# A new order of the steps in a one-core RWKV-7 and GELU kernel, all five engines scheduled by one list

## The chip, the cores and the metric

The kernel runs on one core of a Trainium2 chip. Its time is the device time of one execution in microseconds. Each kernel is run several times and the median counts.

## The reference

Two parts, one behind the other. First a recurrence over 768 time steps, for 4 batches of 8 heads with 40 channels; each head keeps a 40x40 state:

```
for t in range(S):
    y[:, :, t] = einsum('bhd,bhde->bhe', rt, state)
    Sa = einsum('bhde,bhe->bhd', state, at)
    state = state * wt - einsum('bhd,bhe->bhde', Sa, bt) + einsum('bhd,bhe->bhde', vt, kt)
```

Then y, as a matrix x of 3072 tokens by 320, goes through an MLP with 2048 hidden units: `gelu(x @ w_in) @ w_out`, with the exact GELU. Inputs of the recurrence are fp32; w_in and w_out come as 64-bit floats, which the kernel turns into fp32 on the chip.

## The kernel before, in words

The 768 time steps are cut into 12 chunks (c = 0 to 11) of 64. Within a chunk the recurrence is written as matrix products: products of the decayed a, b, k, r and v rows, the inverse of a triangular 64x64 matrix for each of 32 pairs of batch and head, and an update of the state. The MLP for a chunk's 256 tokens comes one chunk later.

Nothing schedules the work but one list. `order` (line 19) returns some 1,470 tokens; the loop at the end of the kernel performs them one by one through `perform` (line 114), and each engine runs its instructions in exactly that order. So a token is a step with its numbers: `sm.7` is step `sm` of chunk 7, `mh.7.2` the step `mh` of chunk 7, part 2. Engines meet through semaphores only. The steps that the text speaks of:

- **Loads, issued by SP**: `Lw La Lb Lk Lr LV Lv Lbt Lwt Lkt` (lines 447 to 486) bring rows of the inputs of a chunk, `Lf` and `Lf5` (537, 547) pieces of w_in, `Ls` (577) of w_out. `ox.c.x` (1241) moves parts of y between halves of the partitions, 5 or 6 DMAs a token, 11 a chunk. `so` and `sz` (1417, 1422) write the output; a last letter `a` or `s` names the queue (ACT or SP).
- **Conversion of the weights**, 18 units u (0 to 9 of w_in, 10 to 17 of w_out). `cp`, `cm`, `cs` on DVE and `ce` on ACT take a unit apart; then either `cv.u` puts it together on DVE (two instructions, lines 636 and 637), or `cl.u` and `cn.u` on ACT and `cg.u` on POOL do it (659, 660). Unit 1 goes over PE (`cx`, `cy`).
- **Decays and transposes**: `lg` `ec` `ew` `lt` `en` on ACT (logarithm and exponentials), `pw` on DVE (a scan), `ta tb tk tr tv tw` transposes (PE and a copy for the first chunks, DVE from chunk 3 on), `sa sb sn kc` on DVE and `sk` on POOL or DVE scale by the decays.
- **Small products on PE**, 32 matmuls each, which the trace counts as 64: `nm vm am` (64 columns), `av xm sm pk pb` (104 columns), `ym` (64), `jm km` (32x32 tiles), and `cu` (the sums of the logarithms).
- **Around them**: `nk vk ak` mask a product on DVE (line 865); `nd` (ACT) and `nx` (DVE) bring the triangular blocks to the tile Nb; `iz` and `ic.c.j0.j1` on POOL invert them in 31 steps of two instructions (962 and 964); `wx` and `tc_` on DVE turn the result, `wa`, `wb` and `jc` on ACT copy. `xc0` and `xc1` (ACT, DVE) copy out behind `xm`, `kt0` and `kt1` behind `km`, `sc.c.g` (DVE, 1176) masks behind `sm`, `yc` (ACT) copies behind `ym`; `oa`, `om`, `od` (DVE) update the state and write y into `xt`, `oc`, `ot` (ACT) and `tn` (DVE) turn the state for the next `ym`.
- **MLP**: `mh.c.p` (1303), 8 a chunk, 10 matmuls each (20 in the trace) of 64 rows with two in the array at once; `ge.c.q` (ACT, 1313) applies GELU to two of them. Then `x W_out` in seven products of half size, `m1` to `m7` (1344), 8 matmuls each (16 in the trace) of the full array, with sums and differences on DVE before (`s1` to `s4`) and behind (`e1` to `e6`, partly ACT). `ws.n` makes the sums of w_out once, on DVE. Chunk 0 uses four plain pieces, `pm.0.n` (1429), instead.
- **warm** tokens are matmuls on constants whose result nobody reads; there are 13 and a first one.

The recurrence goes from chunk to chunk by this path: `od` of the last chunk, `xm`, `xc0`/`xc1`, `sm`, `sc`, `pb`, `oa`, `od`. The inverse of a chunk, `nm` to `nk`, `nd`, `nx`, `ic`, `wx`, `tc_`, `jm`, `km`, `sm`, doesn't need the state and is begun a chunk ahead. PSUM is four tiles that `take` hands out in turn (line 177): a PE step that takes one waits until its last user's readers are done.

Of the kernel before, what the change touches and what calls it, by code (L numbers as in the profile page):

```python
# [18 lines left out]
def order(chunks, first_seven):  # L19
    return """  # L20
        Lw.0 of_half_set warm_set pads_a.1 warm_first pads_a.0 stripes_set Lw.1 bias_set pads_rows.1 pads_VR.1
        sums_mask pads_w.0 pads_extra.3 La.0 pads_VR.0 identity pads_extra.0 first_ones.0 Lf.0.0.0 pads_w.1
        Tt_zero warm.4.5 Lb.0 lg.0 onward_set pads_r.0 lg.1 wT.0 upper_mask Lf.1.1.0 first_ones.1 pads_extra.1
        cu.0 Lf.0.1.0 pads_rows.0 Lf.1.0.0 wT.1 ec.0 Lb.1 ew.0 ta.0 La.1 sb.0 sa.0 tb.0 Lf.3.0.0 Lf.3.1.0 cm.0
        sn.0 cp.0 nm.0 cl.1 Lk.0 warm.4.18 nk.0 Lr.0 cm.1 qi.0.p cu.1 cp.1 cn.1 qt cn.0 warm.4.10 ec.1 qm.0 ew.1
        sb.1 LV.0 parity_set ce.1 qi.1.v cl.0 tb.1 ce.0 cx.1 qz.0 sn.1 qb.0.0.v qc.0 cs.0 cg.0 Lf.2.0.0 qb.0.1.a
        ta.1 cm.3 Lf.0.0.1 cs.1 qm.1 Lf5.1.1 sa.1 pads_extra.2 cy.1 sk.0.p nm.1 qa.1 qz.1 iz.1 tk.0 nk.1 qb.1.1.a
        qc.1 tr.0 qb.1.0.v nd.1 cp.3 kc.0 nx.1 qm.2 Lf.0.1.1 ce.3 ic.1.0.4 rc.0 cs.3 Lw.2 tv.0 cv.3 qc.2 qz.2
        am.0 Lf5.1.0 vc.0 qa.2 ic.1.4.8 qb.2.0.v qb.2.1.a qm.3 Lf.2.0.1 cp.5 ak.0 ce.5 Lf.2.1.1 vm.0 cm.5
        Lf.2.1.0 ic.1.8.12 qz.3 warm.4.6 qa.3 Ls.1 qb.3.0.v warm.4.29 cs.5 vk.0 lg.2 Lk.1 qb.3.1.a cv.5 qc.3 qm.4  # L30
        Lf5.0.1 ic.1.12.16 cp.7 ce.7 av.0 qa.4 cm.2 qx Ls.0 cm.7 cp.2 ql warm.4.21 ic.1.16.20 xc1.0 LV.1
        warm.4.13 ce.2 cs.7 xc0.0 cu.2 cv.7 jm.0 Lf5.0.0 sk.1.v warm.4.8 jc.0 cm.9 warm.4.22 pads_r.1 La.2 km.0
        ic.1.20.24 ec.2 warm.4.24 kt1.0 Lr.1 cs.2 kt0.0 warm.4.3 cv.2 sm.0 Lf.1.1.1 Ls.5 cp.9 warm.4.25
        ic.1.24.28 ce.9 cp.4 sc.0.1 ce.4 pk.0 Lb.2 sc.0.0 cs.9 tr.1 Lf.1.0.1 cm.4 cv.9 Lf.3.1.1 pb.0 rc.1
        unused.v Lf.3.0.1 ic.1.28.31 wT.2 om.0.0 tk.1 om.0.1 od.0.0 ox.0.0 od.0.1 tv.1 cs.4 oc.0 cv.4 ew.2 ta.2
        vc.1 sb.2 cp.6 kc.1 tb.2 unused.a sa.2 ox.0.1 ce.6 am.1 sn.2 cs.6 vm.1 cm.6 ot.0.0 wx.1 nm.2 cv.6 iz.2
        mh.0.0 cm.8 cp.8 Ls.3 ak.1 ce.8 cn.8 cs.8 Ls.7 cl.8 mh.0.1 nk.2 ot.0.1 cg.8 Ls.2 vk.1 wa.1.1 nd.2 mh.0.2
        Lk.2 nx.2 cp.10 ge.0.0 ic.2.0.4 tn.0 av.1 Lr.2 ce.10 cm.10 wa.1.0 ym.1 Ls.4 sk.2.v mh.0.3 yc.1 ic.2.4.8
        cs.10 LV.2 cm.11 tc_.1 tk.2 cp.11 ge.0.1 Ls.11 cv.10 xm.1 ce.11 Ls.6 kc.2 ic.2.8.12 jm.1 cm.12 Ls.9 wb.1
        cp.12 cs.11 mh.0.4 xc1.1 Ls.8 cv.11 xc0.1 jc.1 Ls.10 ce.12 tr.2 cp.13 cs.12 km.1 La.3 rc.2 ic.2.12.16  # L40
        cm.13 tv.2 ce.13 cv.12 kt1.1 Lwt.3 mh.0.6 vc.2 cm.14 cp.14 cs.13 kt0.1 cl.14 cv.13 Lw.3 mh.0.7 ce.14
        cn.14 cs.14 cg.14 am.2 cp.15 cm.15 ce.15 vm.2 Ls.14 mh.0.5 vk.2 ak.2 Ls.15 ic.2.16.20 pm.0.0 cs.15 Ls.13
        cv.15 Ls.12 ge.0.3 ge.0.2 cm.17 Lk.4 ta.3 cn.17 sm.1 ic.2.20.24 tw.3 pm.0.1 lg.3 Lv.3 cp.16 cp.17 sc.1.1
        ce.17 cm.16 ce.16 cs.17 Lr.3 cl.17 sc.1.0 cs.16 pk.1 cv.16 cg.17 pb.1 Lb.3 cu.3 oa.1.1 pm.0.3 ec.3 Lbt.3
        ic.2.24.28 oa.1.0 od.1.1 od.1.0 om.1.1 oc.1 om.1.0 ot.1.1 warm.4.23 ox.1.1 ot.1.0 pc.0.1 ic.2.28.31 av.2
        tn.1 lt.3 ym.2 wx.2 tb.3 pm.0.2 wb.2 yc.2 tc_.2 so.0.1 pw.3 ox.1.0 ew.3 jm.2 pc.0.0 unused.r xm.2 sa.3
        jc.2 wa.2.0 tr.3 km.2 xc0.2 Lk.3 mh.1.0 en.3 wa.2.1 La.4 sn.3 kt1.2 kt0.2 tv.3 nm.3 xc1.2 sk.3.p sm.2
        Lkt.3 nk.3 iz.3 nd.3 mh.1.4 nx.3 sc.2.0 ic.3.0.4 mh.1.5 sc.2.1 ta.4 pk.2 ge.1.2 ic.3.4.8 tk.3 pb.2 Lr.4
        kc.3 mh.1.2 oa.2.1 ws.0 Lbt.4 mh.1.6 ic.3.8.12 ws.1 od.2.1 mh.1.1 Lwt.4 oa.2.0 ws.2 mh.1.3 LV.3 od.2.0
        oc.2 tr.4 ge.1.0 mh.1.7 ws.3 Lw.4 ic.3.12.16 ot.2.0 om.2.0 vm.3 ge.1.3 am.3 ge.1.1 vk.3 so.0.0 m1.1  # L50
        ot.2.1 s1.1 om.2.1 m2.1 ak.3 ox.2.1 ic.3.16.20 tn.2 av.3 s2.1 e1.1 sb.3 ym.3 tb.4 m5.1 yc.3 Lkt.4 tw.4
        ic.3.20.24 m6.1 s3.1 lg.4 e2.1 ox.2.0 s4.1 lt.4 xm.3 pw.4 m3.1 Lb.4 ew.4 ic.3.24.28 xc1.3 m7.1 e3.1 en.4
        e4.1 La.5 tk.4 m4.1 e5.1 ic.3.28.31 Lr.5 sn.4 mh.2.4 e6.1 sa.4 so.1.1 wx.3 mh.2.5 kc.4 wb.3 LV.4 xc0.3
        tc_.3 cu.4 nm.4 Lv.4 ec.4 jm.3 sk.4.p nk.4 mh.2.2 ge.2.2 Lw.5 iz.4 nd.4 wa.3.0 nx.4 mh.2.3 jc.3 wa.3.1
# [1413 lines left out]
```

## Time and profile before

| | us |
|---|---|
| median of the runs (3) | 644.49 |
| lowest, highest | 643.8, 646.84 |
| the profiled execution | 638.89 |
| its span, from first to last instruction | 637.2 |
| PE busy in the span | 621.2 |
| DVE, POOL, ACT busy | 463.5, 383.5, 311.6 |
| first mh step (mh.0.0) begins | 76.2 |
| nm.3 begins | 140.25 |
| last matmul ends | 632.65 |

The times of a profile are those of its one execution, counted from the first instruction. Busy time of PE is that of matmuls; PEld loads their weights and overlaps it. Matmuls are pipelined and their ends are modelled, so the distance from start to start says more than the length of one.

### The profile page before, as it was taken

How to read it: one execution, taken by the hardware profiler on the slowest of the kernel's cores; microseconds unless marked ns; L12 is line 12 of the kernel's file. 1: busy time of each engine (PE TensorE's matmuls, PEld its weight loads, DVE VectorE, ACT ScalarE, POOL GpSimd, SP SyncE). 2: the span in 40 equal slices, each digit the busy share in tenths (PEclk: the TensorE clock that was granted, in tenths of full speed). 3: DMA queues.
4: the chain of work that ended last, by engine and by line, in shares of the span. 5: the costliest groups of instructions: out<-in, count | busy, mean ns of one | idle time of the engine just before them, and what ended most of it. 6: DMA issues, size and time to landing. Idle time of an engine off the chain costs nothing.

```text
span 637.2 us, 27873 instructions
## 1 busy us (share of the span) xinstructions
PE 621.2 (97%) x12424; PEld 548.8 (86%) x12424; DVE 463.5 (73%) x555; ACT 311.6 (49%) x441; POOL 383.5 (60%) x783
## 2 busy tenths in 40 slices
PE   7989999999999999999999999999999999999997
PEld 4676887678998998998988998998998998989996
DVE  1889989989986996986867887984964784833212
ACT  3566684582645454735546536437563275241010
POOL 4568779728867848818958718958918808810000
PEclk9899999999999999999999999999999999999999
DMA  9998587947576458268366466368344440210100
GB/s 152 168 172 162 121 180 160 175 96 123 95 144 114 85 105 149 41 121 143 66 104 116 92 113 123 70 116 153 72 87 96 84 85 4 42 25 3 37 6 21
DMA packets 246898, 64.06 MB, mean 101 GB/s; under 512 B 228380, under 2 KB 243644, under 8 KB 246780
## 3 DMA queue, kind: packets, MB, share of 16 engines
q1 hardware_dynamic: 246340, 62.01, 52.8%
q8 instruction: 97, 1.59, 1.1%
q10 hardware_dynamic: 440, 0.29, 0.2%
q14 instruction: 21, 0.17, 0.1%
HBM read 54.39 MB, written 3.93 MB: 92 GB/s over the span
## 4 chain that ended last, share of the span: by engine, by line
PE 83%; DVE 5%; POOL 3%; ACT 3%; SPq 2%; issue 2%; DMA 1%; DVEq 0%; POOLq 0%; ACTq 0%
PE bank L1308 31%; PE bank L1347 27%; PE bank L194 24%; POOL W L964 2%; POOL tmp L962 2%; DVE conv L628 1%; SPq L447 1%; DMA bk_rows<-in_b_dram 1%; PE bank L1429 1%; SPq L577 1%; DVE SM L1176 1%; DVE conv L636 1%; DMA w_out_sb<-in_moe_w_out_dram 1%; ACT conv L1264 1%; ACT conv L614 0%
## 5 line engine op out<-in xcount | busy, mean ns | idle before, releaser
L1308 PE MATMUL bank<-xt,w_in_sb 64*128 64x256 f32 x1920 | 221.7, 382 | 0.0
L962 POOL TENSOR_TENSOR tmp<-W,Nb 128x126 f32<-128x126 f32 (+22 forms) x341 | 162.4, 476 | 74.4 <-DVE Nb L928 49.0
L1308 PEld LDWEIGHTS bank<-xt,w_in_sb 64*128 64x128 f32 x1920 | 182.0, 187 | 23.2 <-issue 0.8
L964 POOL TENSOR_TENSOR W<-W,tmp 128x126 f32<-128x126 f32 (+22 forms) x341 | 170.7, 501 | 26.7
L1347 PE MATMUL bank<-w_out_sb,gt 128*128 128x160 f32 x704 | 101.1, 301 | 0.0
L1347 PEld LDWEIGHTS bank<-w_out_sb,gt 128*128 128x128 f32 x704 | 96.6, 190 | 2.5 <-issue 1.2
L1313 ACT ACTIVATE gt<-bank 128x1024 f32<-128x1024 f32 x48 | 48.6, 1025 | 85.5 <-PE bank L1308 80.9
L1264 ACT COPY conv<-st 32x128 f32<-32x128 f32 (+2 forms) x55 | 28.0, 509 | 39.5 <-DVE st L1258 31.6
L1176 DVE TENSOR_TENSOR SM<-bank,upper 128x832 f32<-128x832 f32 (+1 forms) x24 | 23.0, 985 | 22.0 <-PE bank L194 21.9
L1300 DVE TENSOR_TENSOR os<-os,bank 128x160 f32<-128x160 f32 x44 | 13.9, 316 | 24.5 <-PE bank L1347 18.2
L1347 PE MATMUL bank<-extra,conv 128*128 128x160 f32 x208 | 30.3, 300 | 0.0
L1300 DVE TENSOR_TENSOR conv<-gt 128x1024 f32<-128x1024 f32 x11 | 14.1, 1286 | 21.6 <-ACT gt L1313 21.6
L1347 PEld LDWEIGHTS bank<-extra,conv 128*128 128x128 f32 x208 | 28.9, 190 | 0.1
L1228 DVE TENSOR_TENSOR st<-bank,st 128x832 f32<-128x832 f32 (+1 forms) x22 | 20.9, 986 | 8.0 <-PE bank L194 8.0
L790 POOL TENSOR_TENSOR bk_rows<-bk_rows,part 128x640 f32<-128x640 f32 x9 | 15.0, 1666 | 19.3 <-DMA bk_rows<-in_k_dram 15.6
L947 POOL MEMSET W<- 128x512 f32 x11 | 5.8, 526 | 34.6 <-DVE Tt L933 34.6
L722 DVE TENSOR_TENSOR_SCAN kT<-spare,kT 128x256 f32<-128x256 f32 x36 | 25.5, 768 | 1.4 <-ACT kT L715 1.4
L1347 PE MATMUL bank<-extra,gt 128*128 128x160 f32 x176 | 25.8, 300 | 0.0
L1347 PEld LDWEIGHTS bank<-extra,gt 128*128 128x128 f32 x176 | 24.5, 190 | 0.1
L1313 ACT ACT_TABLE_LOAD x18 | 23.1, 1283 | 0.3
L1347 PE MATMUL bank<-extra,SM 128*128 128x160 f32 x144 | 21.2, 300 | 0.0
L194 PEld LDWEIGHTS bank<-SM,Tt 64*64 64x64 f32 x768 | 17.2, 133 | 4.1 <-issue 2.3
(218 smaller groups left out, 1113.9 us busy)
## 6 DMA issues: line engine op xcount, KB each, us to landing
bk_rows<-in_b_dram SPq DMA_DIRECT2D x24, 160.0 KB
bk_rows<-in_k_dram SPq DMA_DIRECT2D x24, 160.0 KB
out_dram<-os SPq DMA_DIRECT2D x46, 80.0 KB
VR<-in_v_dram SPq DMA_DIRECT2D x22, 160.0 KB
w_tile<-in_w_dram SPq DMA_DIRECT2D x36, 80.0 KB
a_pairs<-in_a_dram SPq DMA_DIRECT2D x18, 144.0 KB
v_pairs<-in_w_dram SPq DMA_DIRECT2D x18, 144.0 KB
v_pairs<-in_v_dram SPq DMA_DIRECT2D x18, 144.0 KB
```

The costliest lines, as they stand in the source:

```text
L194: nc.tensor.matmul(o, lhsT, rhs, start=first, stop=True, skip_group_check=True)
L722: nc.vector.tensor_tensor_scan(logs[:, at:at + n], onward, logs[:, at:at + n], 0.0, ALU.mult, ALU.add)
L790: (nc.vector if q == "v" else nc.gpsimd).tensor_tensor(to, rows(k_of(c)), decays(c), ALU.mult)
L962: nc.gpsimd.tensor_tensor(t, W[:, BL // 2 - rows:, rest:rest + 1].to_broadcast([P, rows, rest]), Nb[:, rest:rest + 1, :rest].to_broadcast( ...
L964: nc.gpsimd.tensor_tensor(own, own, t, ALU.add)
L1176: nc.vector.tensor_tensor(SM[:, g, :, :, cols], pair_of(f"S{c}_", g).rearrange("p x i c -> p i x c")[:, :, :, cols], kept, ALU.mult)
L1228: nc.vector.tensor_tensor(to, pair_of(f"QY{c}_", g)[:, :, :, cols], to, ALU.add)
L1264: nc.scalar.copy(apart.rearrange("p e i g d -> p (e i g) d")[to_rows, :, to_col:to_col + n], st.rearrange("p e i g c -> p (e i g) c")[rows ...
L1300: nc.vector.tensor_tensor(to, one_, other, how)
L1308: nc.tensor.matmul(ph[:, x, s], w_in_sb[half(x), kt, p * P:(p + 1) * P], xt[half(x), kt], start=kt == 0, stop=kt == NK - 1)
L1313: nc.scalar.activation(gt[:, 4 * q:4 * q + 4].rearrange("p (x s) t -> p x s t", x=2), bank(f"ph{c}_{q}").rearrange("p x (s t) -> p x s t", ...
L1347: nc.tensor.matmul(po[:, n, :DM // 2], l_[:, f], r_[:, f], start=f == 0, stop=f == NF // 2 - 1)
```

## The change

Only the list in `order` changes. Apart from the order of the tokens:

- units 0 and 8 of the weights are now put together on DVE (`cv.0`, `cv.8`), units 2, 6 and 15 on ACT and POOL (`cl`, `cn`, `cg`);
- the warm tokens have other numbers, which are names only; there are still 13 and the first one.

The tokens of the first chunks are in a new order too. The lists of steps on PE from `mh.0.0` on hold the same steps. Some of the lines of the diff, which replaces all 90 lines of the list by 90 others:

```
-        Lw.0 of_half_set warm_set pads_a.1 warm_first pads_a.0 stripes_set Lw.1 bias_set pads_rows.1 pads_VR.1
-        sums_mask pads_w.0 pads_extra.3 La.0 pads_VR.0 identity pads_extra.0 first_ones.0 Lf.0.0.0 pads_w.1
-        Tt_zero warm.4.5 Lb.0 lg.0 onward_set pads_r.0 lg.1 wT.0 upper_mask Lf.1.1.0 first_ones.1 pads_extra.1
-        cu.0 Lf.0.1.0 pads_rows.0 Lf.1.0.0 wT.1 ec.0 Lb.1 ew.0 ta.0 La.1 sb.0 sa.0 tb.0 Lf.3.0.0 Lf.3.1.0 cm.0
-        sn.0 cp.0 nm.0 cl.1 Lk.0 warm.4.18 nk.0 Lr.0 cm.1 qi.0.p cu.1 cp.1 cn.1 qt cn.0 warm.4.10 ec.1 qm.0 ew.1
...
-        ic.1.20.24 ec.2 warm.4.24 kt1.0 Lr.1 cs.2 kt0.0 warm.4.3 cv.2 sm.0 Lf.1.1.1 Ls.5 cp.9 warm.4.25
-        ic.1.24.28 ce.9 cp.4 sc.0.1 ce.4 pk.0 Lb.2 sc.0.0 cs.9 tr.1 Lf.1.0.1 cm.4 cv.9 Lf.3.1.1 pb.0 rc.1
-        unused.v Lf.3.0.1 ic.1.28.31 wT.2 om.0.0 tk.1 om.0.1 od.0.0 ox.0.0 od.0.1 tv.1 cs.4 oc.0 cv.4 ew.2 ta.2
-        vc.1 sb.2 cp.6 kc.1 tb.2 unused.a sa.2 ox.0.1 ce.6 am.1 sn.2 cs.6 vm.1 cm.6 ot.0.0 wx.1 nm.2 cv.6 iz.2
...
-        cn.14 cs.14 cg.14 am.2 cp.15 cm.15 ce.15 vm.2 Ls.14 mh.0.5 vk.2 ak.2 Ls.15 ic.2.16.20 pm.0.0 cs.15 Ls.13
-        cv.15 Ls.12 ge.0.3 ge.0.2 cm.17 Lk.4 ta.3 cn.17 sm.1 ic.2.20.24 tw.3 pm.0.1 lg.3 Lv.3 cp.16 cp.17 sc.1.1
-        ce.17 cm.16 ce.16 cs.17 Lr.3 cl.17 sc.1.0 cs.16 pk.1 cv.16 cg.17 pb.1 Lb.3 cu.3 oa.1.1 pm.0.3 ec.3 Lbt.3
...
-        ic.8.8.12 mh.6.4 Lbt.9 wa.7.1 km.7 Lk.8 mh.6.1 kt1.7 pw.9 ic.8.12.16 kt0.7 LV.8 sm.7 ge.6.0 Lkt.9 tb.9
-        mh.6.5 sc.7.1 sc.7.0 pk.7 ic.8.16.20 ge.6.2 s1.6 pb.7 LV.9 cu.8 oa.7.1 m1.6 oa.7.0 ec.8 od.7.0 ic.8.20.24
...
-        ge.11.1 mh.11.5 m1.11 ge.11.2 s1.11 m2.11 s4.11 s2.11 m5.11 e1.11 s3.11 e2.11 m3.11 m6.11 m7.11 e4.11
-        e3.11 m4.11 e5.11 so.11.0 sz.11.0.1.a e6.11 sz.11.1.0.a sz.11.0.0.s sz.11.1.1.a
+        Lw.0 pads_extra.3 warm_set pads_extra.0 warm_first identity pads_extra.1 sums_mask Lf.1.0.0 Lw.1 pads_w.1
+        pads_r.0 pads_a.1 Tt_zero Lb.0 pads_a.0 bias_set first_ones.1 pads_r.1 of_half_set warm.4.13 La.0
+        first_ones.0 pads_w.0 lg.0 pads_VR.0 upper_mask wT.0 pads_rows.0 stripes_set Lf.0.1.1 lg.1 warm.4.0
+        Lf.0.1.0 cu.0 Lf.0.0.0 Lf.1.1.0 warm.4.1 ec.0 La.1 wT.1 ew.0 sb.0 tb.0 Lb.1 sn.0 ta.0 cu.1 Lf.3.0.0
+        warm.4.20 ec.1 Lk.0 cm.0 ew.1 cp.0 sa.0 Lf.3.1.0 parity_set iz.1 cp.1 nm.0 cm.1 ce.1 pads_VR.1 warm.4.12
...
+        ak.0 ic.1.12.16 qm.4 Lk.2 ce.2 vk.0 tr.1 Lf.1.1.1 qa.4 Lf5.1.0 ql ic.1.16.20 lg.2 cs.5 jm.0 cv.5 av.0
+        jc.0 Ls.0 cs.2 km.0 xc0.0 cp.7 Lk.1 xc1.0 ce.7 cu.2 kt0.0 ic.1.20.24 qx kt1.0 warm.4.9 LV.1 cm.2 cs.7
+        warm.4.18 cm.7 warm.4.19 cv.7 Lb.2 rc.1 sm.0 cn.2 cp.9 Ls.5 cm.9 pads_rows.1 ce.9 warm.4.29 cg.2 sc.0.0
+        La.2 sk.1.v pk.0 ec.2 sc.0.1 cl.6 Lf.3.1.1 cs.9 pb.0 ic.1.24.28 cv.9 tk.1 Ls.1 om.0.1 tv.1 om.0.0 od.0.1
+        Ls.4 od.0.0 wT.2 cp.4 sb.2 ic.1.28.31 ce.4 warm.4.25 ox.0.1 vc.1 cm.4 cs.4 tb.2 kc.1 sk.2.v ta.2 cv.4
+        ew.2 am.1 sn.2 unused.a cp.6 vm.1 oc.0 sa.2 ce.6 wx.1 ot.0.1 nm.2 ox.0.0 cm.6 iz.2 cs.6 cn.6 nk.2 ot.0.0
+        unused.v mh.0.0 ak.1 nd.2 cg.6 wa.1.1 nx.2 Lf.3.0.1 tn.0 Ls.3 ic.2.0.4 Ls.6 mh.0.1 cp.8 cm.8 LV.2 ce.8
...
+        ce.14 Ls.12 cl.15 am.2 cs.14 cg.14 mh.0.5 Ls.14 ak.2 cm.15 Ls.13 vk.2 cn.15 pm.0.0 Ls.15 cp.15 tw.3 ce.15
+        Lr.3 cs.15 cg.15 ge.0.3 cm.16 ge.0.2 ta.3 sm.1 ic.2.20.24 cp.16 Lbt.3 ce.16 cm.17 pm.0.1 cp.17 cl.17
+        cs.16 ce.17 sc.1.0 cn.17 sc.1.1 cs.17 cv.16 cg.17 pk.1 lg.3 lt.3 pb.1 Lb.3 cu.3 oa.1.1 Lk.3 pm.0.3
+        ic.2.24.28 ec.3 oa.1.0 od.1.1 LV.3 od.1.0 om.1.1 oc.1 om.1.0 ot.1.0 sk.3.p ox.1.1 warm.4.21 ot.1.1 pc.0.1
+        av.2 tn.1 ic.2.28.31 sb.3 ym.2 pm.0.2 yc.2 wx.2 tc_.2 iz.3 so.0.1 wa.2.1 pw.3 wb.2 ox.1.0 ew.3 jm.2
...
+        km.7 mh.6.5 kt1.7 kt0.7 tr.9 sb.7 Lkt.9 sm.7 ge.6.2 ic.8.12.16 pk.7 sc.7.0 LV.8 sc.7.1 cu.8 pb.7 s1.6
...
+        ge.11.1 m1.11 ge.11.2 s1.11 m2.11 s2.11 s4.11 m5.11 s3.11 m6.11 m3.11 e3.11 e1.11 e2.11 e4.11 m7.11 m4.11
+        e5.11 so.11.0 sz.11.1.1.a e6.11 sz.11.0.1.a sz.11.0.0.s sz.11.1.0.a
```

From `mh.0.0` on there are 307 steps on PE in both lists. Steps of one array shape that stand side by side make a run; the shapes are those of mh (64 rows by 128 columns), of m and pm (128 by 128), of the small products (64 rows) and of jm and km (32 rows).

## The prediction

> **What bounds the kernel now.** I read the page's first two parts first: busy time by engine, and the 40 slices.
>
> ```profile
> span 637.2 us, 27873 instructions
> PE 621.2 (97%) x12424; PEld 548.8 (86%) x12424; DVE 463.5 (73%) x555; ACT 311.6 (49%) x441; POOL 383.5 (60%) x783
> PE   7989999999999999999999999999999999999997
> DVE  1889989989986996986867887984964784833212
> ```
>
> PE is the bound, with 16.0 us of idle time in 637.2. To find where the idle time lies I asked for the busy time of stretches (the first figure behind the stretch is its length, the second PE's busy time, the fourth DVE's).
>
> ```profile
> 0.00:20.00 20.00, 14.28 (x222) 9.16 (x223) 4.01 (x6) 7.24 (x8) 7.42 (x42) 0.87 0.96 152
> 20.00:76.00 56.00, 52.20 (x1375) 40.53 (x1376) 53.49 (x78) 34.38 (x48) 41.73 (x79) 0.99 0.83 155
> 76.00:140.00 64.00, 62.10 (x1281) 50.12 (x1270) 57.83 (x73) 45.37 (x64) 42.91 (x68) 1.00 0.73 151
> 140.00:300.00 160.00, 160.00 (x3320) 145.00 (x3318) 131.72 (x144) 80.71 (x113) 113.33 (x233) 1.00 0.65 116
> 600.00:637.20 37.20, 32.63 (x272) 30.34 (x268) 8.21 (x16) 4.88 (x7) 0.00 (x0) 0.98 0.08 19
> ```
>
> Idle PE: 5.7, 3.8 and 1.9 us in the first three, none from 140 us on until the end (4.6 us after the last matmul). So there are three accounts: a start up to about 140 us, in which DVE is busy 53.49 of 56 us and sets the pace; a middle in which PE never stops, so that only PE's own work can shrink; and a tail. The change moves no matmul out of the program, so the middle can gain only from the order's effect on a matmul's price.
>
> The chain of waits shows that effect (start, length, line, count):
>
> ```profile
> 280.64 6.68 PE bank L1308 x60
> 289.10 4.52 PE bank L1308 x40
> 294.30 2.36 PE bank L1308 x20
> 306.51 15.41 PE bank L1347 x112
> ```
>
> One mh step is 20 matmuls. One, two and three of them cost 2.36, 4.52 and 6.68 us: 2.16 each and 0.20 for the run. By start-to-start distances in the timeline of PE, a step whose neighbour has another array shape costs 0.10 more on each side for mh and m, 0.05 (before) and 0.11 (behind) for the small products; jm and km, at 32 rows, also count as another shape.
>
> **The change, part by part.** Tokens were mapped to instructions by counting each engine's instructions in its own order.
>
> *Shape changes in the middle.* From mh.0.0 on, both lists hold the same 307 PE steps. The runs of small products between MLP work fall from 65 to 62. At 0.36 us for a run (0.20 for the MLP run that it cuts, 0.16 for itself) this would be -1.1 us. But direct changes between mh and m or pm rise from 9 to 12, those between 64-row and 32-row small steps from 13 to 15, and all changes of shape from 155 to 156. Entries into MLP work and exits from it go from 75 to 76 each, those of small steps stay at 80 each: 2 x 0.10 = **+0.2 us**. The Trainium skill (TensorEngine Tiling (Array Packing), Key Properties) says that a change of tiling mode, not of the tile alone, drains the engine. By a count of small runs alone the sum would have -1.1 us here; by the page's rule the direct changes between mh and m count too, and the row agrees: m4.1 to mh.2.4 is 2.26 us, against 2.17 between two m steps.
>
> *Waits in the middle.* For each PE step from chunk 3 on I added up the PE work between what starts a chain and its consumer, and the work of the DVE or ACT queue between them. No pair of the new list is short. The nearest: pb.7 needs both sc.7 (2 x 0.98 us on DVE) and has pk.7 and cu.8 before it (1.48 + 0.65): 0.1 us left. In the old list the nearest are 0.1 to 0.5 us too, and PE idles 0.0 us. I take **0**; bounds 0 and +4 (the slower rival). It can't be below nothing, since no wait is there to remove.
>
> *The inverse on POOL.* From the end of nm.c to tc_.c the traced chunks took 42.1 us at best (chunk 4: 34.8 us of POOL steps, 7.3 us around them). The PE work between nm.c and jm.c in the new list is 48.4, 44.6, 47.8, 52.8 us for chunks 3 to 6, later ones over 51; before, 48.4, 47.1, 56.4, 59.4. All stay above 42.1.
>
> *The start.* (a) DVE. Two units of conversion come to DVE (cv.0, cv.8), three leave (cv.2, cv.6, cv.15): 1.58 + 1.19 + 1.85 us by their own rows, and the two that come at 1.5 each: -1.6 us. DVE's work ahead of nk.2 falls from 58.9 to 56.0 us, ahead of tn.1 from 103.3 to 101.7, ahead of the last thing that nm.3 waits for (sn.3 before, sa.3 now) from 112.5 to 111.5. The waits that this can shorten:
>
> ```profile
> PEld bank L194 <- DVE SM L1176: 1.1, 1, 1.1
> PEld bank L194 <- DVE turned L1279: 0.9, 1, 0.9
> ```
>
> They are pb.1 and ym.2; PE's own idle time is 0.90 and 0.69 us, and 0.31 before pm.0.0: the 1.9 us of the stretch from 76 us. (b) SP. mh.0.0 needs ox.0.0 and ox.0.1, whose 11 DMAs SP issues one after another:
>
> ```profile
> 61.19 5.27 SPq L537 DMA_DIRECT2D gt<-in_moe_w_in_dram  x4
> 67.27 0.90 SPq L1246 DMA_DIRECT2D xt<-xt  x1
> ...
> 72.72 2.46 SPq L1249 DMA_DIRECT2D xt<-xt  x4
> ```
>
> The last goes out at 75.18 and mh.0.0 starts at 76.19. SP is never idle for long before: it ends the loads at 66.46 and waits 0.8 us for om.0. The new list puts Lk.2 (2.36 us of issue) and Ls.4 (1.35) ahead of ox.0 and takes Lf.3.0.1 (0.65) away: +3.1 us, less the 0.8 us of waiting = +2.3 for mh.0.0; with the shortest issues of these kinds (0.47 to 0.67 us each) +0.9. PE's 1.9 us of idle time behind mh.0.0 takes most of that up, if DVE is 1.3 to 1.6 us further in its queue. Value for the start **-0.3 us**, between -1.0 (0.9 - 1.9) and +0.4 (2.3 - 1.9). Outer bounds: -2.9 (the whole lead of DVE), +3 (2.3 with nothing absorbed, and jm.2 late by under 1: POOL has cg.6, cg.14, cg.15 and cg.17 between nm.2 and wx.2, 5.8 us more work than before, and cg.17 waits there for DVE anyhow, which hides most of it). (c) ACT gets one unit more (1.6 us in all) and two fewer table loads by the order of its functions (47 for 49, 1.28 us each); ACT is busy 34.4 of 56 us, so both count as nothing; without that cover, 1 us either way.
>
> *The tail.* Column, source and count of the last DMAs:
>
> ```profile
> 631.87 2.54 ACTq L1422 DMA_DIRECT2D out_dram<-os  x3
> 632.67 0.32 DVE L1300 TENSOR_TENSOR os<-os,bank 128x160 f32<-128x160 f32 x1 [0.83 <-PE bank L1347]
> 633.02 0.47 SPq L1422 DMA_DIRECT2D out_dram<-os  x1
> ```
>
> ACT issues three: one before e6, then two behind it (633.03 and 633.56, the last done at 634.41); the last one's packets end the transfers at 635.42. In the new list only one of the three needs e6, and the other two go ahead. The last issue then starts at 633.03 in place of 633.56: -0.53 to -0.88 us. I take **-0.7**.
>
> *Sum.* +0.2 + 0 - 0.3 - 0.7 = **-0.8 us**. The profiled execution took 638.89 us (span 637.2, 1.7 around it); the median of the runs is 644.49, 5.6 above it, and their spread is 643.8 to 646.84. On the median: 643.7.
>
> **Rivals.** (1) *The lead of the start comes through* (faster). For it: DVE sets the pace up to 130 us, its work ahead of nk.2 is 2.9 us less, and b's first rows are issued 2.2 us sooner (Lb.0 ends at 6.4 us of SP work, before at 8.6), where DVE's first step waited 11.9 us for them. Against it: SP's longer way to ox.0, and nm.3, where the lead is down to 1.0. Time: -2.9 + 0.2 - 0.7 = -3.4, 641.1.
>
> (2) *The inverse comes late* (slower). The steps on POOL take far longer beside some DVE work:
>
> ```profile
> 310.58 1.23 POOL L962 TENSOR_TENSOR tmp<-W,Nb 128x96 f32<-128x96 f32 x1
> 317.55 0.33 POOL L962 TENSOR_TENSOR tmp<-W,Nb 128x70 f32<-128x70 f32 x1
> ```
>
> The first of these ran beside a DVE add of two operands from memory (1.41 us at 310.17), the second in a gap of DVE. The same 62 steps took 32.8 to 40.4 us by chunk (47.3 in chunk 2, with two conversion units among them). The new order gives chunk 4 the least room, 44.6 us: from 44.6 - 7.3 = 37.3 us of steps on, PE stands at jm.4 and everything behind it moves. At 41 us in chunks 3 to 5 the waits are 0, 3.7 and 0.5: +4.2 - 0.8, 647.9. Against it: chunk 4 took 34.8, and its POOL queue has 2.5 us less work ahead of wx.4 than before. The Trainium skill (SBUF — State Buffer, SBUF: two separate sides) calls the pair of ports of VectorE and GpSimd an exclusive lock, held for a whole instruction. By that rule each collision costs up to one DVE instruction, which the rows at 310 us bear out; where they fall in a new order can't be read from the old trace.
>
> (3) *The change isn't what it says.* It is not: the new list has 4 to 7 runs of small products a chunk, as the old one (4 to 7), not three. With three in each of 11 chunks, 33 for 62, 29 runs fewer would be worth 29 x 0.36 = 10 us; this is not in the list, so the time stays that of the forecast.
>
> **Chances and range.** Forecast, start within its inner bounds or a little beyond: 0.48. Rival 1 and what lies beyond it: 0.27. Rival 2, or the start's loss in full together with it: 0.25. About 0.5% (3.2 us) is what a measurement here tells from no change; so faster 0.27, same 0.48, slower 0.25. Range: down to 640 (rival 1 and 1 us of idle PE saved with it), up to 649 (rival 2 and 1 us of the start).
>
> **What would show it.** Middle: PE busy 100% from 140 us, mh steps still 2.16 us, 156 changes of shape. Wrong if waits at jm.3 to jm.5 appear, or at pb.7 and pb.10. Start: mh.0.0 at 77 to 78.5 us behind ox.0.0, and no idle time at pb.1 and ym.2. Tail: the last ACT DMA issued at some 0.4 us behind the start of e6. The forecast falls if PE's idle time between 140 us and the last matmul is over 3 us, or if nm.3 starts more than 3 us from 140.25.

## Result and profile after

| | before | after |
|---|---|---|
| median of 15 executions (us) | 644.06 | 649.10 |
| lowest, highest | 639.36, 646.84 | 643.68, 652.91 |
| span of the profiled execution | 637.2 | 644.5 |
| mh.0.0 begins | 76.19 | 78.44 |
| nm.3 begins | 140.25 | 145.85 |
| m4.11 begins | 630.30 | 638.09 |
| from m4.11 to the end | 6.88 | 6.38 |

The ratio of the times is 1.0086, 95% interval 1.0063 to 1.0108: slower by 0.9%, where -0.1% was forecast; 649.1 is just outside the range of 640 to 649. In the experiments below, executions that took over 1.5% longer than the fastest of their kernel are left out.

The page of the changed kernel (its span; busy time by engine; three rows of the 40 slices):

```profile
span 644.5 us, 27882 instructions
PE 623.7 (97%) x12424; PEld 550.6 (85%) x12424; DVE 463.1 (72%) x553; ACT 310.5 (48%) x441; POOL 389.4 (60%) x785
PE   8889998999999999999999999999999999999997
DVE  0888998989988887776975976986877775833312
PEclk9897999999999999999999999999999999999999
```

PE still bounds the kernel, but it stands idle for 20.8 us instead of 16.0, and PEclk shows a fall of the granted clock at 48 to 64 us. Busy time by stretch (columns: length; PE, PEld, DVE, ACT, POOL busy; granted clock, DMA share, GB/s):

```profile
0.00:20.00 20.00, 14.20 (x166) 8.26 (x166) 3.04 (x5) 8.31 (x9) 7.45 (x39) 1.00 0.92 150
20.00:76.00 56.00, 52.63 (x1368) 42.06 (x1368) 50.52 (x73) 32.68 (x46) 40.98 (x76) 0.91 0.89 159
76.00:140.00 64.00, 58.49 (x1130) 46.68 (x1121) 57.25 (x69) 40.69 (x59) 50.52 (x80) 1.00 0.64 140
140.00:300.00 160.00, 159.20 (x3405) 144.69 (x3408) 130.56 (x146) 80.56 (x115) 102.54 (x208) 1.00 0.61 112
600.00:644.50 44.50, 40.43 (x328) 37.95 (x326) 9.06 (x18) 5.25 (x10) 0.00 (x0) 0.98 0.07 16
```

DVE has the lead that was forecast: it has done 55.65 us of work when nk.2 starts, before 59.41. But nk.2 starts no sooner (78.00 us, before 77.83). In the stretch from 20 us DVE is not full any more (50.52 us busy, before 53.49), and ahead of that it stands longer for a first piece of w_in. Its waits for such pieces (total, times, longest), changed and before:

```profile
DVE conv L621 <- DMA w_out_sb<-in_moe_w_in_dram: 5.4, 1, 5.4
```

```profile
DVE conv L621 <- DMA w_out_sb<-in_moe_w_in_dram: 0.9, 1, 0.9
```

From 76 us on PE idles 5.5 us, before 1.9. What its weight loads wait for there:

```profile
PEld bank L1429 <- DVE late L865: 2.8, 1, 2.8
PEld bank L194 <- issue: 2.1, 7, 0.4
PEld bank L194 <- ACT gt L1313: 1.8, 1, 1.8
```

The waits at pb.1 and ym.2 are gone, as forecast; in their place stand pm.0.0 (2.42 us of idle PE, for the mask ak.2) and sm.1 (1.59 us, for a GELU). SP's way to ox.0 and the tail:

```profile
67.00 3.11 SPq L577 DMA_DIRECT2D w_out_sb<-in_moe_w_out_dram  x4
70.22 2.80 SPq L1246 DMA_DIRECT2D xt<-xt  x2
73.06 2.75 SPq L1249 DMA_DIRECT2D xt<-xt  x4
...
76.66 2.41 SPq L1249 DMA_DIRECT2D xt<-xt  x4
```

```profile
639.59 1.86 ACTq L1422 DMA_DIRECT2D out_dram<-os  x3
640.47 0.32 DVE L1300 TENSOR_TENSOR os<-os,bank 128x160 f32<-128x160 f32 x1 [0.90 <-PE bank L1347]
640.81 0.47 SPq L1422 DMA_DIRECT2D out_dram<-os  x1
```

ox.0 starts at 70.22 us, before at 67.27. The second half of om.0, for which it waits, ended at 69.72 instead of 67.24 us (+2.5), and Ls.4, the last two DMAs of the first line, held SP 0.5 us longer behind it. PE itself also came later to mh.0.0: the step ahead of it, nm.2, ended at 77.87 us instead of 76.26. Only the new kernel then waits for ox.0 (mh.0.0 before, then changed):

```profile
76.19 4.15 PE L1308 MATMUL bank<-xt,w_in_sb 64*128 64x256 f32 x35
```

```profile
78.44 5.92 PE L1308 MATMUL bank<-xt,w_in_sb 64*128 64x256 f32 x49 [0.57 <-DMA xt<-xt]
```

In the tail the last of ACT's issues starts 0.4 us behind the start of e6, as forecast, and ends 0.98 us behind it (before 1.74).

One profile of each kernel says +5.6 us up to nm.3, +2.2 from nm.3 to m4.11, -0.5 in the tail. The experiments below brought more traces of each part; in this table every kernel counts whose order is that of before or of the changed kernel in the whole part, unless its whole list changes over at the start of the part.

| part | old order, us | new order, us | difference |
|---|---|---|---|
| to mh.0.0 | 76.2 to 78.8, mean 77.4 (5 traces) | 78.4 to 84.2, mean 80.0 (6) | +2.6 |
| mh.0.0 to nm.3 | 64.1 to 68.5, mean 66.3 (9) | 65.0 to 67.4, mean 65.9 (8) | -0.3 |
| nm.3 to m4.11 | 490.0 to 492.1, mean 490.8 (10) | 491.8 to 493.6, mean 492.7 (6) | +1.9 |
| m4.11 to the end | 6.9 to 7.3, mean 7.0 (9) | 6.0 to 6.7, mean 6.4 (9) | -0.7 |

So the +3.4 us that the first two profiles show between mh.0.0 and nm.3 were chance: the first trace of before was the shortest of its kind there, and that of the changed kernel the longest. Every trace is one execution; the scatter in the first row leaves the +2.6 a standard error of 1.0 us.

### The profile page after: what moved, and what is told of

It is laid out like the page before. It is cut to its first block, busy times and chain, and to the rows that moved or that the text cites. A ratio compares the mean times of both kernels' runs of the same rounds, so it can differ in the third digit from the quotient of the medians.

```text
span 644.5 us, 27882 instructions
## 1 busy us (share of the span) xinstructions
PE 623.7 (97%) x12424; PEld 550.6 (85%) x12424; DVE 463.1 (72%) x553; ACT 310.5 (48%) x441; POOL 389.4 (60%) x785
## 3 DMA queue, kind: packets, MB, share of 16 engines
q8 instruction: 97, 1.59, 1.1%
## 4 chain that ended last, share of the span: by engine, by line
PE 76%; SPq 8%; DMA 5%; DVE 4%; POOL 2%; ACT 2%; issue 2%; DVEq 0%
PE bank L1308 31%; PE bank L1347 27%; PE bank L194 19%; SPq L447 4%; SPq L577 2%; DMA bk_rows<-in_k_dram 2%; DMA w_out_sb<-in_moe_w_out_dram 1%; DMA a_pairs<-in_a_dram 1%; POOL W L964 1%; POOL tmp L962 1%; DVE conv L628 1%; SPq L537 1%; DVE conv L636 1%; SPq L486 0%; SPq L1249 0%
## 5 line engine op out<-in xcount | busy, mean ns | idle before, releaser
L964 POOL TENSOR_TENSOR W<-W,tmp 128x126 f32<-128x126 f32 (+22 forms) x341 | 168.1, 493 | 26.7
L1300 DVE TENSOR_TENSOR conv<-gt 128x1024 f32<-128x1024 f32 x11 | 15.4, 1400 | 19.8 <-ACT gt L1313 19.8
L722 DVE TENSOR_TENSOR_SCAN kT<-spare,kT 128x256 f32<-128x256 f32 x36 | 23.7, 717 | 2.3 <-ACT kT L715 2.3
L194 PEld LDWEIGHTS bank<-SM,Tt 64*64 64x64 f32 x768 | 17.1, 133 | 6.0 <-issue 3.1
L614 ACT ACTIVATE conv<-conv,rebias 128x512 uint16<-128x512 uint16 (+1 forms) x18 | 13.7, 769 | 17.0 <-DVE conv L607 16.9
L194 PE MATMUL bank<-SM,Tt 64*64 64x104 f32 (+1 forms) x768 | 19.6, 250 | 1.6 <-ACT gt L1313 1.6
```

Of the source, the lines that this page charges most:

```text
L194: nc.tensor.matmul(o, lhsT, rhs, start=first, stop=True, skip_group_check=True)
L722: nc.vector.tensor_tensor_scan(logs[:, at:at + n], onward, logs[:, at:at + n], 0.0, ALU.mult, ALU.add)
L964: nc.gpsimd.tensor_tensor(own, own, t, ALU.add)
L1300: nc.vector.tensor_tensor(to, one_, other, how)
```

## Experiments

Each kernel was timed beside the kernel before on the same chip. A diff shows places in the list. In the first four kernels the list takes two lines fewer; L192 in them is L194 of the others.

### The kernel before once more, and halves of both lists

> The kernel before, unchanged, so that the granted TensorE clock of each of its executions is known. In the 15 executions of the changed kernel the clock was 0.984 to 1.00 of full speed; lost time, (1 - clock) x span, is 6.1 us on the mean, and the time rises by 0.78 us for each us lost. Theory 'clock' (the changed order leaves PE idle at one place more in the start, and the clock drops there): the kernel before loses 2 to 4 us on the mean, some 3 less than the changed one. Theory 'waits' (loads and DVE are later, the clock is the same): it loses 6 us too, and the difference of 5 us stays at equal clocks.

> The old list up to nm.3, and from there all remaining steps in the new order. Theory 'start' (the start is the step of the prediction that failed: nm.3 came 5.6 us later): nm.3 at 140 to 141 us in the profile, time 643 to 645.5, as the kernel before. Theory 'middle' (the new order costs PE time in the middle, shape changes or waits): m4.11 comes over 2 us later behind nm.3 than the old list's 490.05 us, time 647 to 649.

> The new list up to nm.3, and from there all remaining steps in the old order. Theory 'start': nm.3 at 145 to 146.5 us, time 648 to 650, as the changed kernel. Theory 'middle': time 643 to 645 although nm.3 is late, since the old order takes up what the new one can't.

```
 start_of_before: the old list to nm.3, then
-tokens from nm.3 on in the old order
+all tokens that are left, in the new order
 start_of_after: the reverse
```

Measured: before 641.81 (kernel before beside it 641.83), start_of_before 645.26, start_of_after 646.86. Both halves cost: +3.4 and +5.0 us; the sum is more than the whole, since the seams bring waits of their own (1.0 and 1.8 us of idle PE behind nm.3). Neither "start" nor "middle" is the only place.

Lost clock, (1 - clock) x span: 4.4 us on the mean of 104 executions of the kernel before, 6.1 in the 15 of the changed one. The time rises by 0.63 us for each us lost in the one and 0.78 in the other, and a straight line through each gives 638.9 and 644.3 us at full clock. So the clock explains about 1 us of the 5, and much of the scatter; the theory "clock" alone falls.

### A warm matmul where PE stood idle

> The changed kernel with one more warm matmul (512 columns) directly ahead of qm.4, where PE was idle for 1.39 us at 45 us; the granted clock was 0.5 to 0.7 from 48 to 56 us behind it. Theory 'clock': the idle time ahead of qm.4 falls under 0.5 us, the clock stays at 1.00 from 44 to 60 us, mh.0.0 begins at 75.5 to 77 us in place of 78.44, and the median falls by 1 to 3 us. Theory 'waits' (Lk.2 and Ls.4 ahead of ox.0, and DVE's order, set mh.0.0): mh.0.0 stays at 78 to 79 us whatever the clock is, and the time stays within 1 us.

```
-ic.1.12.16 qm.4
+ic.1.12.16 warm.4.24 qm.4
```

Measured 647.11 us, mh.0.0 at 78.68, as "waits" had it. The idle time ahead of qm.4 is gone and the clock stays full behind it, but PE now stood 1.09 us at nm.1 and 2.10 us at tv.0, and behind the second the clock was half from 40.4 to 43.8 us. The two waits are of the kind "issue": no engine and no DMA of the profile releases them. The new start has them in most traces, here start_of_after:

```profile
34.25 1.11 PE L192 MATMUL bank<-aT,nT 40*64 40x64 f32 x32 [1.88 <-issue]
...
43.99 1.03 PE L192 MATMUL bank<-ident,VR 128*64 128x128 f32 x12 [2.25 <-issue]
```

Both cut a step in two (nm.1 and tv.0, which began at 31.65 and 40.43 us), where a wait for these steps' operands would lie ahead of the step. And they lie at fixed places of PE's instruction count (matmuls and weight loads), whatever step stands there: 1,459 lies in am.0 in the new order of PE and in qm.3 in the old.

| instructions ahead of the idle time | traces | idle, us | a block landed ... us before its end |
|---|---|---|---|
| 699 | 5 new | 0.4 to 2.7 | 1.4 to 1.9 |
| 951 or 953 | 6 new (one of them new to qm.0 alone), 1 old | 0.8 to 2.8 | 1.3 to 1.9 |
| 1,205 | 4 new | 1.6 to 2.3 | 1.5 to 1.8 |
| 1,459 | 3 new, 1 with PE and SP old | 0.4 to 1.9 | 1.4 to 1.8 |
| 1,715 | 6 new | 0.5 to 1.4 | 1.3 to 1.5 |
| 2,989 | 3 old | 0.7 to 1.1 | 1.2 to 1.4 |
| 20,069 to 20,075 | all 9 with the new middle | 0.4 to 1.9 | 1.2 to 1.5 |

The kernel old_new_PE_SP (below) is left out; it stands at the first four places too, 0.4 to 2.7 us. The first five stand 252 to 256 apart (the count takes matmuls and weight loads alone). The page's third part has the queue that brings them (packets, MB, share):

```profile
q8 instruction: 97, 1.59, 1.1%
```

97 packets of 16 KB for 24,848 matmuls and weight loads are 256 instructions each: PE's own program. The Trainium skill (Runtime: NRT & Kernel Launch, Instruction fetch mechanics) says the same size, and that the next block is fetched while the current one runs, so that crossing a block's end is mostly hidden; the size agrees, and at the ends in the table it is not hidden. In all 20 traces PE never passed the end of a block sooner than 1.2 us behind the landing of the next one.

### Does the gap in the middle belong to a step or to an instruction number?

> The changed kernel with one more warm matmul (512 columns, about 1.0 us of PE work, 4 instructions) directly ahead of km.9. In the three traces with the new middle PE stands still for 1.0 to 1.13 us within mh.8.2, at 492 us, waiting for nothing that the profile shows; a 16 KB block on the instruction queue had landed 1.25 to 1.5 us before the end of that gap, behind the stretch with the most PE instructions of the whole list (1,153 in 16 us). Theory 'instructions' (PE has run through its instructions faster than they are brought): the added microsecond is for nothing, the gap falls to 0.0 to 0.3 us, and the distance from jm.9 to sm.9 (11.1 us) grows by at most 0.2. Rival 'wait' (mh.8.2 waits for its operands, whatever stands ahead of it): the gap stays about 1 us, and the distance grows by 1.0.

> The changed kernel with 32 small matmuls on constants (64 rows, 32 columns, which the trace counts as 64, with 64 weight loads) ahead of km.9, at the place where one wide matmul of about 1.0 us and 4 instructions was tried: about the same time on PE or less, 32 times the instructions. From jm.9 to sm.9 it took 11.1 us without and 12.78 us with the wide matmul. Theory 'instructions' (behind this stretch PE waits for its next block of 256 instructions): 13.3 to 15 us, and the gap within mh.8.2, or another one close by, grows from 1.05 to 1.5 to 3 us. Rival (operands): 11.8 to 12.8 us, the gap stays at 1.0 to 1.2.

```
-km.9
+warm.4.24 km.9          (warm_at_km9: one matmul of 512 columns)
+warm.0.24 km.9          (thin_at_km9: 32 matmuls of 32 columns)
```

The changed kernel, warm_at_km9 and thin_at_km9 in turn (PE's timeline):

```profile
492.48 0.70 PE L1308 MATMUL bank<-xt,w_in_sb 64*128 64x256 f32 x4
494.31 0.92 PE L1308 MATMUL bank<-xt,w_in_sb 64*128 64x256 f32 x6 [1.13 <-issue]
```

```profile
494.19 1.13 PE L1308 MATMUL bank<-xt,w_in_sb 64*128 64x256 f32 x8 [1.05 <-issue]
```

```profile
492.77 0.22 PE L194 MATMUL bank<-T,Js 32*32 32x32 f32 x2 [0.40 <-issue]
493.42 0.70 PE L1312 MATMUL bank<-xt,w_in_sb 64*128 64x256 f32 x4
```

The sizes failed both theories. From jm.9 to sm.9 it took 11.10 us in the changed kernel, 12.78 with the wide matmul (the gap did not shrink) and 12.36 with the thin ones, which took 1.95 us on PE. The place decides: 128 more instructions ahead of mh.8.2 move the gap out of mh.8.2 and into km.9, and in each of the three kernels it begins behind instruction 20,073. In the thin kernel, all blocks behind it being shifted by 128, two new gaps appear at 539 and 580 us (0.56 and 1.52 us), each 1.35 to 1.45 us behind a landing. So the gap belongs to the block, and the rival "operands" falls. Why the microsecond of the wide matmul was not won: the block started at 491.7 us although PE passed the last block's end 1.1 us sooner than without it; SP had issued LV.10 at 491.5 (494.3 without it), and the DMA engines' share from 491 to 493 us was 1.2 and 1.0 for 0.68 and 0.70. That a load held the block up is argued from this, not shown.

Times: warm_at_km9 646.77 (before 641.33), thin_at_km9 650.12, one execution.

### Single moves in the new start

> The changed kernel with sa.0 ahead of cm.0 and cp.0 on DVE. There DVE stood 5.4 us for the first pieces of w_in, and sa.0, nm.0 and PE (2.7 to 3.1 us idle) behind it. Theory 'instructions' (nm.0 comes late, so nm.0, qm.0, qm.1 and nm.1, 640 instructions, follow each other closer than their blocks can be brought): nm.0 starts at 16 to 18 us in place of 20.2, the gaps at the ends of blocks 3 to 7 (1.4 to 5.2 us in the three traces with the new start) fall to under 1 us, nm.3 comes 1.5 to 4 us earlier and the time falls by 1.5 to 3 us. Rival 'later work sets the pace' (DVE's queue behind it is as long as before): nm.0 earlier, but jm.0 and mh.0.0 as before (78 to 79 us), time within 1 us of the changed kernel.

> The changed kernel with Ls.7 directly behind Ls.6 on SP (it was issued at 94.3 us, in the old list at 77.2, and DVE's cp.13 stood 2.7 us for it). Theory 'late load': PE's waits at pm.0.0 (DVE, 2.4 us) and sm.1 (ACT, 1.6 us) fall to under 1.5 us together, nm.3 comes 67 us or less behind mh.0.0 + 0 (67.4 in the changed kernel, 64.1 in the first trace of before), and the time falls by 1 to 3 us. Rival 'no effect': the traces of the old start have 3.1 to 3.4 us of idle time at pm.0.0 as well, in two of three; the waits at pm.0.0 and sm.1 stay at 2 to 4 us together and the time within 1 us.

> The changed kernel with Lf5.0.1 and Lf5.1.1 (four DMAs each, used from 62 us on) behind Lr.1 on SP, so that LV.0, Lr.0, Lf.2.0.0, Lf.1.0.1, Lf.2.1.0 and Lr.1 go out 2 to 4 us sooner. In nine of twelve traces with the new list ahead of qm.0, PE's block 2 or 3 was brought 4 to 6 us after PE had passed the end of the block before (in all five of the old list 1.1 to 2.3 us). Theory 'order of the loads' (these pieces ahead of Lr.0 hold up the block and DVE's rows): delays of blocks 2 and 3 under 3 us, waits at nm.1 and tv.0 under 0.5 us, time 1.5 to 3 us below the changed kernel, 2 to 4 us above the kernel before. Rival 'load as a whole' (DMA queues are full in any order): the delays stay at 4 to 6 us, time within 1 us of the changed kernel, 5 to 6.5 us above the kernel before.

```
 sa0_first
-cm.0 ew.1 cp.0 sa.0
+ew.1 sa.0 cm.0 cp.0
 Ls7_early
-Ls.3 ic.2.0.4 Ls.6 mh.0.1 ... Ls.9 ce.11 Ls.7
+Ls.3 ic.2.0.4 Ls.6 Ls.7 mh.0.1 ... Ls.9 ce.11
 Lf5_later
-Lf5.0.1 ... LV.0 ... Lf5.1.1 ... Lr.0 ... Lr.1
+LV.0 ... Lr.0 ... Lr.1 Lf5.0.1 Lf5.1.1
```

Measured 647.52 and 647.78 us (before 641.33) and 650.32 (before 641.06; 5 executions, 644.85 to 652.75; ratio 1.0112, 1.0060 to 1.0164). No move wins anything. sa0_first: nm.0's wait is gone, but PE then stood 2.65 us at instruction 699, and mh.0.0 came at 80.31. Ls7_early: no wait at pm.0.0 and 0.19 us at sm.1, as "late load" had it, but mh.0.0 itself came at 80.66 and the time didn't fall; the old order idles 2.0 to 3.4 us at pm.0.0 as well, in five of the ten traces that have it there. Lf5_later: the delays of blocks 2 and 3 are 5.2 and 4.1 us, as the rival "load as a whole" had it. Its clock shows what can follow a standstill (columns as above):

```profile
44.00:48.00 4.00, 2.10 (x92) 1.96 (x88) 3.86 (x7) 2.21 (x4) 3.53 (x7) 0.99 0.92 130
48.00:52.00 4.00, 3.99 (x87) 2.92 (x86) 4.00 (x6) 3.59 (x5) 3.45 (x8) 0.50 1.09 203
52.00:56.00 4.00, 4.00 (x65) 3.45 (x64) 0.07 (x1) 0.75 (x2) 3.37 (x9) 0.50 0.88 186
...
64.00:68.00 4.00, 4.00 (x36) 2.63 (x31) 2.53 (x6) 3.22 (x7) 1.39 (x6) 0.50 1.12 145
```

After 1.9 us of standstill PE ran at half its clock for some 20 us, though it was busy throughout. The changed kernel's own trace has the smaller form:

```profile
44.00:48.00 4.00, 2.61 (x52) 1.75 (x53) 2.92 (x6) 2.17 (x4) 3.37 (x9) 1.00 1.05 134
48.00:52.00 4.00, 3.73 (x81) 3.29 (x79) 3.90 (x6) 2.02 (x2) 3.45 (x8) 0.60 0.79 164
52.00:56.00 4.00, 4.00 (x116) 3.69 (x112) 2.67 (x5) 1.91 (x4) 3.53 (x7) 0.55 0.82 170
```

The Trainium skill (TensorE: Matmul & The Clock Gate, What's actually happening) has the clock halved after an idle window of about 3.4 us and full again after a busy one. The two values agree. Here 1.4 and 1.9 us of standstill came ahead of the fall, and a busy PE stayed at half clock for some 20 us. But a standstill of this length doesn't always bring a fall: the granted clock stayed 1.00 behind 1.50 us at qm.3 (39 us) in the profile before and behind the 2.42 us at pm.0.0 in the changed one. What decides it stays open.

### One queue at a time, and where in the start

> The kernel before; only SP's queue ahead of mh.0.0 has the new order (34 of its places differ), every other engine its old one. mh.0.0 started at 76.2 to 78.3 us in four traces of the old start (mean 77.05), at 78.4 to 84.2 in six of the new one (mean 80.2). Theory 'loads' (the new order of the loads makes their pieces and PE's instruction blocks late): mh.0.0 at 79 to 82 us, time 1.5 to 3.5 us above the kernel before. Theories 'PE order' and 'DVE order': mh.0.0 at 76 to 78.5 us, time within 1 us of the kernel before.

> The kernel before; only PE's queue ahead of mh.0.0 has the new order (41 places). Theory 'PE order' (it sets how closely PE's instruction blocks follow each other): in three or more of blocks 1 to 5 PE passes the end less than 2 us behind the landing of the next block, as in the new start (in the old start in none or one of them), mh.0.0 at 79 to 82 us, time 1.5 to 3.5 us above the kernel before. Theories 'loads' and 'DVE order': mh.0.0 at 76 to 78.5 us, time within 1 us, apart from waits that the old order of the other engines brings to moved PE steps (named in the trace).

> The kernel before with both queues, PE's and SP's, in the new order ahead of mh.0.0; DVE, ACT and POOL as before. If PE and SP together make the loss of the start: mh.0.0 at 79 to 82 us, time 2 to 4 us above the kernel before. Theory 'DVE order' (the order of conversions and scalings on DVE, ACT and POOL sets it): mh.0.0 at 76 to 78.5 us, time within 1 us.

> The changed kernel with PE's and SP's queues ahead of mh.0.0 in the old order; DVE, ACT and POOL in the new one, as all that follows. Theory 'DVE order': mh.0.0 stays at 79 to 82 us and the time 4 to 6 us above the kernel before. If PE and SP make the loss: mh.0.0 at 76 to 78.5 us and the time 1.5 to 3 us above the kernel before, which is what the middle and the tail of the new list are worth by their traces (+2.3 and -0.5).

```
 old_new_SP: ahead of mh.0.0, SP's tokens alone (Lk.2 and Ls.4 stay behind it)
-Lw.0 Lw.1 La.0 Lf.0.0.0 Lb.0 Lf.1.1.0 Lf.0.1.0 Lf.1.0.0 Lb.1 La.1 Lf.3.0.0 Lf.3.1.0 Lk.0 Lr.0 LV.0 ...
+Lw.0 Lf.1.0.0 Lw.1 Lb.0 La.0 Lf.0.1.1 Lf.0.1.0 Lf.0.0.0 Lf.1.1.0 La.1 Lb.1 Lf.3.0.0 Lk.0 Lf.3.1.0 Lf5.0.1 LV.0 ...
```

Measured (before 642.75): 646.68, 659.18, 659.36 and 654.50 us. PE's order alone doesn't bear another order on DVE: in old_new_PE it stands 8.2 us at tr.1, and the three kernels with it tell nothing of the change. SP's order alone brings 3.9 us to the old list, with mh.0.0 at 81.80. None of PE's waits ahead of mh.0.0 lies at the end of a block in this trace: the loads cost here by coming late for the engines, and part of that is the same misfit (what its weight loads wait for, 20 to 85 us):

```profile
PEld bank L194 <- issue: 5.3, 18, 0.8
PEld bank L752 <- issue: 4.0, 4, 3.2
PEld bank L194 <- ACT st L1044: 3.2, 2, 2.4
PEld bank L194 <- DVE st L1001: 3.2, 1, 3.2
```

> The new list up to qm.0, and from there all remaining steps in the old order. By the traces so far qm.0 starts at the same time in both (23.5 us old, 23.8 new, means), and the whole difference of the start (3.1 us at mh.0.0) comes between jm.0 and mh.0.0. Theory 'last part' (it is made by what the new order does from jm.0 on): mh.0.0 at 76 to 78.5 us, time within 1 us of the kernel before. Theory 'from the first block on' (the first 25 us leave DVE or PE's instruction blocks behind): mh.0.0 at 79 to 82 us, time 2 to 4 us above the kernel before.

> The new list up to jm.0, then the old order. Theory 'last part': mh.0.0 at 76 to 78.5 us, time within 1 us of the kernel before, apart from waits at the seam. Theory 'from the first block on', or 'DVE is behind at jm.0 already': mh.0.0 at 79 us or later, time 2 to 4 us above.

> The new list up to mh.0.0, then the old order. All theories that put the loss of the start ahead of mh.0.0: mh.0.0 at 79 to 82 us, time 2 to 4 us above the kernel before. Rival (the loss comes between mh.0.0 and nm.3, from Ls.7 and the waits at pm.0.0 and sm.1): mh.0.0 the same, time within 1 us of the kernel before.

```
 new_to_qm0: the new list to qm.0, then
-tokens from qm.0 on in the new order
+all tokens that are left, in the old order
 new_to_jm0, new_to_mh0: the same at jm.0 and mh.0.0
```

Measured (before 640.12): 644.02, 649.18 and 647.28 us; mh.0.0 at 79.07, 84.48 (with 3.83 us of idle PE at pk.0, behind the seam) and 79.82. "From the first block on" holds, if barely: the first 25 us of the new list bring 3.9 us between the medians (2.8 by the ratio, 1.0044, 1.0020 to 1.0068), although qm.0 starts at 24.30 us, in the old start at 22.1 to 24.7. Some of it may be the seam: PE waits 2.3 us for operands at qm.3 and qm.4. It also stands at instruction 953, in nm.1:

```profile
35.48 0.69 PE L194 MATMUL bank<-aT,nT 40*64 40x64 f32 x32 [2.67 <-issue]
```

With SP's new order ahead of qm.0, block 2 started 3.8 us or more behind PE's passing the last block's end in 10 of 13 traces (1.4 to 7.4 us), with the old one in 1 of 7 (1.9 to 2.3, once 6.5). The changed kernel's own trace is one of the three others of the 13 (1.8 us).

### A better one of both

> The kernel before with the order of the last output DMAs from the new list, nothing else. The prediction's tail of -0.7 us: from the start of m4.11 to the end of the span 6.2 us in place of 6.88; the whole time 0.4 to 0.9 us below the kernel before, which 5 rounds may not tell from nothing. Rival (the transfer that ends last is another one, the step is worth nothing): 6.8 to 7.0 us. It is also one more look at the old start: nm.3 at 140 to 146.5 us, and no instruction gap at the ends of PE's blocks 3 to 7.

> A try at a version that beats both: the kernel before with the new tail, and with cp.15, cm.15 and ce.15 behind vk.2 and ak.2. In four of five traces of the old start PE stood 2.3 to 3.4 us at pm.0.0 for the mask vk.2, which lay behind these conversions on DVE (2.6 to 3.6 us with both). If nothing else is late, pm.0.0 waits under 1 us and the time falls by 1 to 2.5 us below the kernel before, with 0.5 of it from the tail; if the conversions of the second half of w_out are late instead, the wait moves to pb.1 or pm.0.3 and only the tail's 0.5 us is left.

```
 old_with_new_tail
-so.11.0 sz.11.0.1.a e6.11 sz.11.1.0.a sz.11.0.0.s sz.11.1.1.a
+so.11.0 sz.11.1.1.a e6.11 sz.11.0.1.a sz.11.0.0.s sz.11.1.0.a
 old_vk2_first: this, and
-cp.15 cm.15 ce.15 vm.2 Ls.14 mh.0.5 vk.2 ak.2
+vm.2 Ls.14 mh.0.5 vk.2 ak.2 cp.15 cm.15 ce.15
```

Measured 641.26 (before 641.33; tail 6.24 us) and 640.16 (before 641.06; ratio 0.9987, 0.9967 to 1.0007). The tail's 0.6 us are in the trace, and the wait at pm.0.0 is gone from it. old_vk2_first is the fastest version, but its interval takes in no change.

## Why the prediction was wrong

- **Middle, shape changes, +0.2.** Right in direction; no run tests the kind. PE's own work from nm.3 to m4.11, without idle time, is 491.1 us on the mean of the new order's traces and 490.5 of the old one's: +0.6, with 0.5 us of scatter in each.
- **Middle, waits, 0.** Wrong: +1.4. The inverse was in time, as worked out (jm.c came 0.7 us or more behind tc_.c in every chunk, rival 2 did not happen), and pb.7 and pb.10 do not wait. km.4 waits 0.31 us for ACT's jc.4, and the gap at instruction 20,073 is 0.7 to 1.9 us where PE reaches it unhindered, mean 1.2. The working compared engine with engine; it had no term for PE's instructions. By the trace, the new order has 1,153 of them in the 16 us ahead of the gap, and the old list at most 1,070 in any 16 us. The count alone doesn't decide it: another 16 us of the changed kernel, from 531.4 us, hold 1,148 and bring no gap.
- **Start, -0.3.** This is the step that failed, by its sign and size: +2.6 us. The forecast's own sign came, nm.3 at 145.85 us, more than 3 us from 140.25. (a) DVE's lead is real, 3.8 us at nk.2, but goes unused, since DVE waits for late loads (5.4 us for a piece of w_in, 2.7 at cp.13). (b) mh.0.0 came +2.25, inside the forecast +0.9 to +2.3, by luck: the path was wrong. The working took mh.0.0 to start when ox.0 is there; in all five traces of the old start it follows nm.2 on PE without idle time. In five of the six of the new start it waits for ox.0, 0.5 to 1.3 us, mean of the six 0.7; the other 1.9 us is PE reaching the end of nm.2 later. Nor was ox.0 late by SP's longer way alone, 0.5 us: om.0 itself was 2.5 us late. Nothing absorbed it. In the place of SP's way the runs show standstills of PE at the ends of its instruction blocks, ahead of mh.0.0: 0.5 to 6.0 us, mean 3.2, in six traces of the new start, 0 to 2.8, mean 1.1, in five of the old. That is 2.0 of the 2.6 us. No run took these standstills away by themselves, so the sum is argued from the traces; and old_new_SP loses as much without them.
- **Tail, -0.7.** Right in mechanism; -0.5 us in the first two profiles, and -0.6 in the old list with the new tail alone.
- **Rivals.** None of the three. "The change isn't what it says" stays right: no gain of 10 us was in the list. The slower rival was looked for on POOL, where the rows showed a price, and not among the loads, which the working counted as SP time only. That PE's instructions can arrive late, and more often with SP's new order, was in no rival.
- What stays open: why block 2 is late in most traces with the new order of the loads and not with the old. The move of the pieces that stood out (Lf5_later) didn't help. About 1.4 us of the difference between the medians are in no part of the table; the lost clock (6.1 us for 4.4, at 0.65 us each) would be of that size.

## What to carry to other kernels

Where PE is the bound and steps are made of many small matmuls, count PE's instructions as a resource: waits named "issue" that cut a step in two, at the same instruction number whatever stands there, are its blocks coming late. Bundling small products makes stretches dense in instructions. That queues full of loads delay the block is likely by these traces, but no run shows it alone. And one trace of a start that scatters by 3 us is no base for terms of 1 us: take the same stretch from several.

## What the runs showed of the hardware

- PE passes the end of a block of 256 instructions no sooner than 1.2 us behind the landing of the next one; between passing a block's end and the next block's start on the DMA queue lay up to 8.2 us in the starts (old_new_PE_SP), with the DMA engines' share near 1.
- Standstills of 1.4 to 1.9 us were followed by half the granted clock for 7 us (the changed kernel) and 20 us (Lf5_later), with PE busy; standstills of 1.50 us (before, 39 us) and 2.42 us (changed, 109 us) were not.
- The 104 executions of the kernel before lie between 637.7 and 646.7 us. A full clock would give 638.9 by the line through them, 2.5 us less than their median of 641.4.
